# Gate arithmetic in a PSUM bank, reciprocals in spare PSUM columns, and another order of all steps, in a fused sparse-attention and mixture-of-attention-experts kernel

## The chip, the cores and the metric

The kernel runs on one core of a Trainium2 chip. A core has five engines with their own instruction queues: TensorE (matmuls, PE in the profile, its weight loads PEld), VectorE (DVE), ScalarE (ACT), GpSimd (POOL) and SyncE (SP). Here SP issues the loads of v and the stores of the output, and GpSimd issues the loads of q, k and the weights. Matmul results land in PSUM, which has eight banks of 512 float32 columns on 128 partitions; GpSimd works on SBUF only in this kernel. The metric is the device time of one launch in microseconds (us); lower is better.

## The reference

Two stages. The first is an attention for 4 batches, 8 heads, 768 positions and 64 columns, in which each query sees its neighbours within 16 positions and 24 block summaries (the maximum of k and the mean of v over blocks of 32). Its output, seen as 768 rows of 512 columns per batch, is the input x of the second stage: four attention experts, of which each row uses the two with the largest gate logits.

```python
k_sum = k.reshape(B, H, nb, block, D).max(axis=3)
v_sum = v.reshape(B, H, nb, block, D).mean(axis=3)
scores_l = scale * np.matmul(q, k.transpose(0, 1, 3, 2))      # kept where |i - j| < 16
scores_s = scale * np.einsum('bhsd,bhnd->bhsn', q, k_sum) + np.log(block)
# softmax over both, times [v, v_sum]
...
logits = x @ w_gate                                           # (B, S, 4)
topk = np.argpartition(-logits, K, axis=-1)[..., :K]          # K = 2
w = softmax of the two selected logits
for e in range(E):
    q, k, v = x @ wq[e], x @ wk[e], x @ wv[e]
    a = causal softmax of scale * q @ k.T
    ye = a @ v @ wo[e]
    out += (weight of expert e in each row) * ye
```

## The kernel before

Every piece of work is a step with a name, a function that issues its instructions, and the buffers that it reads and writes. `make_plan` lists the steps; `TABLE` is an order written out by hand: one entry per step with its number, its engine (P, V, A, G, S for TensorE, VectorE, ScalarE, GpSimd, SP) and the slots of the buffers that are new in it. `emit` issues the steps in that order, so each engine works through its own steps in the order of the table, and a step waits for data and for buffers. The durations beside each step (`{"V": 0.65}`) take no part in what is issued.

Names carry batch, pair of heads or of experts, and part. First stage, for batch b and pair of heads c (16 times): dk, dq, dv load (lines 285, 303); kz zeroes the spare rows of the three `kn` buffers (line 214); tk and tq transpose k and q on TensorE (line 393); rk takes the block maxima (410), kw and cq copy the transposed k and q out of PSUM, ksc appends the maxima; bs and be sum v over blocks (322, 340) and ds spreads the sums into `vb`, and hc copies v's overlapping halves; for four groups of heads (`TREE`), tr does the sums by additions on GpSimd (367, 370), on the buffer `vt` that vtz zeroes once; sc makes scores (435 the mask, 441 the product), ex exponentiates (449), av multiplies with v (459), rc and xm divide, tx transposes (486), hi and lo split the result into two half-precision parts (503 is lo).

Second stage, for each batch: vp multiplies x with the values' weights and the gate's (554, 557) for two of six row blocks at a time, lg copies the eight gate columns out to `lgp`, v2 copies the values out; then the gate, on 24 numbers per partition: ga (583 to 586) joins the logits' two parts, takes the maximum and subtracts; gx exponentiates on ScalarE (590); gb (595 to 598) finds the second largest and a mask; gc (603 to 606) makes the weights. All of these work in the SBUF buffer `gt`. For each pair of experts cc: pp makes q and k (622), pc copies them out, sp makes scores in six units (646), es exponentiates (654), dm zeroes the upper triangle on GpSimd (659), aw multiplies with the values (670). Then r2 (689, 691) takes the reciprocal of the softmax sum and multiplies it with the gate's weight, wv scales the result into `wav` (696), tw transposes (708), ct copies to `wT`, op multiplies with the output weights (728), oc copies out and od stores (739). The last batch splits r2 to ct into row blocks 0 to 3 and 4 to 5.

PSUM buffers are numbered slots of one tensor of eight banks; most second-stage buffers take two neighbouring banks. Some steps have a filler in front of them (`f...`): three matmuls on zeros in the same bank, issued if the table gives it to P and left out if it gives N.

The gate's weight columns hold two parts: `cg` (533 to 536) rounds the gate weights to half precision and stores the remainder times `LO_SCALE` (2048).

Of the kernel before, what the change touches and what calls it, by code (L numbers as in the profile page):

```python
# [55 lines left out]
95,A, 92,P,0 96,A, 115,P,1 45,N,2 98,P,0 117,V, 46,P,2 33,N,5 119,V, 50,V, 247,G,0 49,V, 99,A, 248,G,2 47,V, 34,P,1
35,V, 54,N,0 120,N,2 259,G,0 51,N,6 32,A, 68,P,4 28,A, 17,S,2 66,N,5 55,P,1 56,A, 103,N,0 12,V, 52,P,2 137,G, 53,A,
118,G, 136,G, 14,G, 67,P,0.1 36,A, 71,V, 69,P,2 19,N,6 20,P,0 21,V, 121,P,3 100,P,6 140,G, 73,A, 72,G, 122,A, 138,G,
22,G, 15,G, 74,N,2 101,P,4 70,V, 313,P,4.1.0 37,S,3 75,P,5 438,G,1 433,S,0 104,P,0.0 434,G, 139,G, 435,G,0 249,S,4
18,V, 102,A, 77,N,6 24,A, 78,P,0 315,A, 79,A, 39,N,5 40,P,1 142,V, 105,P, 41,V, 42,A, 316,V, 269,N,6 270,P,0.2  # L60
59,P,4.1.1 57,N, 106,V, 107,V, 274,V, 58,P, 60,V, 292,N,7 61,V, 76,A, 123,N,0 16,V, 124,P,4 293,P,2.1 297,V, 275,A,
62,N,4 63,P,0.0 38,A, 125,A, 296,V, 64,A, 80,N,2 108,N,0 109,P,1.1 110,V, 111,V, 82,P,1.2 81,P, 294,P,7 65,V,
126,N,0 127,P,0.0 273,A, 128,P, 331,P,6.0 83,V, 251,S,5 84,V, 129,V, 130,V, 295,P,2 299,A, 271,N,7 85,N,4 159,N,2
86,P,2.2 87,A, 88,V, 131,N,0 132,P,3.3 133,A, 134,V, 335,V, 272,P,1 276,A, 277,N,4 160,P,0 280,N,0 281,P,1 282,A,
161,V, 278,P,2 162,N,6 169,N,0 163,P,1 164,V, 317,A, 279,A, 330,P,2.0.2 333,V, 332,A, 314,P,3.1 318,V, 143,N,6
144,P,0.0 146,V, 439,G,1 427,G,0 145,V, 165,N,4 166,P,0 167,A, 321,P,2.0 322,A, 170,P, 334,A, 171,A, 253,N,6 254,P,0
298,G, 255,V, 181,N,4 303,N,2 304,P,5 177,N,0 178,P, 300,N,6 301,P,3 256,V, 305,A, 151,N,2 152,P, 302,A, 179,A,
154,A, 153,V, 185,N,6 186,P, 252,G, 436,G,1 187,A, 338,P,0.4 339,A, 173,N,2 182,P, 174,P, 257,V, 307,P,6.1.1 175,A,
262,S,2 250,V, 306,P, 308,V, 309,V, 483,P,0.2.0 486,V, 183,A, 485,V, 336,P,2.5 337,A, 310,P,6.4.4 311,V, 319,P,4.3
444,S,0 188,G, 500,P,1.0.2 445,G, 320,A, 200,N,2 201,P,2 197,N,4 198,P,0 312,V, 487,V, 260,S,0 219,N,6 202,V, 199,A,  # L70
147,N,2 264,N,0 503,V, 265,P,1 180,G, 266,V, 502,A, 220,P,1 221,A, 148,P, 484,P,4.2 267,V, 449,P,5.1.1 285,P,0.0.2
172,G, 268,A, 150,V, 452,V, 453,V, 283,N, 284,P, 451,A, 263,G, 341,P,6.1.0 340,P, 488,V, 149,A, 211,N,4 446,G,1
428,G,2 450,P,2.0 454,A, 286,V, 287,V, 501,P,3.1 212,P, 489,P,0.1 342,V, 343,V, 447,G,3 505,V, 344,P,6.5.5 345,V,
491,P,2.2 213,A, 346,V, 261,G, 323,P,4.1.1 324,P, 490,A, 492,A, 455,P,6.4 456,A, 325,V, 326,V, 288,N,0 289,P,6.6
290,V, 457,P,2.5 458,A, 223,N,6 224,P, 327,P,4.7.7 207,N,2 208,P, 225,A, 291,V, 328,A, 209,A, 467,P,6.2 471,V,
466,P,7.2.0 168,G, 597,G,2 329,V, 504,G, 469,V, 448,G,5 215,N,0 216,P, 203,N,2 636,P,6.1.1 639,V, 176,G, 217,A,
204,P, 362,P,4.1 470,A, 363,V, 360,P,0.0 431,S,4 155,V,0 184,G, 205,A, 389,P,4.2 598,G,0 468,A, 474,P,2.3 156,A,
361,V, 440,S, 157,V, 614,S,0 640,G, 189,P,0.0.0 141,G, 432,G, 390,V, 158,V, 191,P, 190,P, 192,V, 638,A, 367,P,4.0
193,V, 475,A, 472,P,6.0 368,A, 364,P,0 441,G, 494,P,2.0.2 493,P, 473,A, 365,A, 437,G, 506,P,4.2 495,V, 496,V,
620,P,6.0 507,A, 619,P,7.2.2 379,P,0 621,V, 218,G, 370,P,2 380,A, 371,A, 381,G, 622,V, 376,P,4 377,A, 222,G, 624,V,  # L80
214,G, 347,P,0.1.1 349,A, 348,V, 353,P,2 497,P,4.0.0 355,V, 498,V, 206,G, 373,P,6 374,A, 499,V, 391,P,0.0 442,S,
443,V, 429,S, 369,G, 226,G, 210,G, 227,P,1.1.6 228,P, 392,A, 229,P, 230,V, 231,V, 354,A, 408,P,4.1 409,A, 393,P,0
396,P,6 402,P,2 394,A, 476,P,4.1.0 403,A, 397,A, 477,P, 601,S,2 430,G, 478,V, 479,V, 399,P,0 400,A, 350,P,2 352,V,
623,G, 351,V, 608,G,1 508,P,6.1 509,A, 404,G, 480,P,4.1.1 627,P,0.0 628,A, 609,G,1 481,V, 482,V, 405,P,2 406,A,
460,P,6.0.1 459,P, 461,V, 462,V, 670,P,0.0.0 672,A, 637,P,1.2 641,A, 232,N,4 233,P,0 234,V, 625,P,2.3 626,A, 673,V,
# [791 lines left out]
```

## Time and profile before

| What | us |
| --- | --- |
| Median of three runs | 203.48 (203.15 to 208.5) |
| Profiled execution, its own time | 205.5 |
| Its span, first to last instruction | 203.6 |
| First instruction to end of the first batch's last lo | 50.0 |
| End of the last projection (pp301) | 184.9 |

The span is divided among engines in busy time, and the same span is followed back from its last instruction as a chain: at each step to what released it. An instruction's wait is shown in brackets with its releaser. The tile `gt` is the gate's buffer; `wav` holds the scaled attention output; `ps` is PSUM; a line can be a helper's, such as 181 for any copy on VectorE or GpSimd and 179 for any on ScalarE.

### The profile page before, as it was taken

The page shows a single profiled execution, that of the slowest core. Times are in us where ns is not written, and L with a number is a line of the kernel's source. Part 1 is how long each engine was busy: PE and PEld are TensorE (multiplying, and loading weights), DVE is VectorE, ACT ScalarE, POOL GpSimd, SP SyncE. Part 2 cuts the span into 40 slices and gives each one's busy share as a digit, 9 for nine tenths or more (in the row PEclk, how much of TensorE's full clock was granted, in tenths as well). Part 3 has the DMA queues.
Part 4 walks back from the last instruction along what each step waited for, and adds up shares of the span by engine and source line. Part 5 has one row for each costly group of instructions (what it writes and reads, how often), then busy time and mean ns, then how long its engine had stood idle before and what let it go on. Part 6 is the DMA issues. An engine that isn't in the chain of part 4 may idle for free.

```text
span 203.6 us, 7088 instructions
## 1 busy us (share of the span) xinstructions
PE 160.1 (79%) x3071; PEld 117.2 (58%) x3071; DVE 133.2 (65%) x251; ACT 121.9 (60%) x158; POOL 100.1 (49%) x156
## 2 busy tenths in 40 slices
...
GB/s 46 201 207 178 191 173 73 77 209 140 83 198 172 16 3 159 187 205 163 122 3 3 77 85 105 164 284 46 11 95 3 3 3 310 3 3 0 217 215 190
DMA packets 44207, 23.54 MB, mean 116 GB/s; under 512 B 33168, under 2 KB 39568, under 8 KB 44176
## 3 DMA queue, kind: packets, MB, share of 16 engines
...
HBM read 24.13 MB, written 6.29 MB: 149 GB/s over the span
## 4 chain that ended last, share of the span: by engine, by line
PE 37%; DVE 23%; POOL 13%; DMA 13%; issue 6%; ACT 4%; SPq 1%; ACTq 0%; DVEq 0%; POOLq 0%
DMA vt<-in_v_dram 9%; PE ps L459 8%; PE ps L622 5%; PE ps L670 4%; PE ps L728 4%; PE ps L554 3%; DVE wav L696 3%; PE ps L646 3%; DMA qn<-in_q_dram 3%; POOL kn L214 3%; POOL vt L367 2%; DVE ks L410 2%; DVE kw L181 2%; PE ps L393 2%; PE ps L486 2%
## 5 line engine op out<-in xcount | busy, mean ns | idle before, releaser
L654 ACT ACTIVATE a<-ps 128x1024 f16<-128x1024 f32 (+1 forms) x48 | 42.6, 923 | 13.6 <-PE ps L646 10.1
L659 POOL TENSOR_SCALAR_AFFINE_SELECT a<-a 128x256 f16<-128x256 f16 x48 | 18.7, 415 | 59.1 <-ACT a L654 42.4
L449 ACT ACTIVATE aT<-ps 120x768 f32<-120x768 f32 x32 | 25.7, 813 | 19.0 <-PE ps L441 18.9
L459 PE MATMUL ps<-vb,aT 120*64 120x65 f32 x768 | 28.4, 233 | 0.8 <-DVE vs L340 0.3
L459 PEld LDWEIGHTS ps<-vb,aT 120*64 120x64 f32 x768 | 25.8, 146 | 4.2 <-issue 2.4
L622 PE MATMUL ps<-hi,wqk 128*128 128x384 f16 x128 | 23.9, 340 | 0.4 <-DVE lgp L181 0.4
L646 PE MATMUL ps<-qk,qk 64*128 64x512 f16 (+3 forms) x128 | 16.5, 320 | 9.2 <-DVE wav L696 6.6
L367 POOL TENSOR_TENSOR vt<-vt 120x1024 f32<-120x1024 f32 (+1 forms) x8 | 14.6, 1820 | 17.0 <-DMA vb<-in_v_dram 9.7
L410 DVE TENSOR_REDUCE ks<-ps 128x24 f16<-128x768 f16 x16 | 15.0, 948 | 10.0 <-PE ps L393 10.0
L179 ACT COPY kw<-ps 128x1152 f16<-128x1152 f16 x10 | 11.1, 1119 | 14.8 <-DVE ks L410 14.4
L435 PE MATMUL ps<-pi,mt 64*128 64x384 f16 x64 | 12.8, 377 | 7.4 <-DVE wav L696 5.0
L622 PEld LDWEIGHTS <-wqk 128*128 128x128 f16 x128 | 12.4, 101 | 9.8 <-issue 3.1
L503 DVE TENSOR_TENSOR lo<-ps,hi 128x768 f16<-128x768 f32 x16 | 15.0, 954 | 1.4 <-ACT hi L179 0.9
L474 DVE TENSOR_TENSOR x<-ps,rec 128x768 f32<-128x768 f32 x16 | 15.3, 957 | 0.5
L441 PEld LDWEIGHTS <-kw 64*128 64x128 f16 x384 | 12.1, 104 | 5.1 <-issue 3.2
L670 PE MATMUL ps<-v,a 128*128 128x65 f16 x336 | 13.0, 199 | 2.3 <-ACT ob L179 1.1
L670 PEld LDWEIGHTS <-a 128*128 128x128 f16 x336 | 12.5, 101 | 4.0 <-issue 2.8
L441 PE MATMUL ps<-qT,kw 64*128 64x64 f16 x384 | 13.3, 204 | 1.4 <-issue 1.4
L554 PE MATMUL ps<-wvg,hi 128*128 128x264 f16 x96 | 13.8, 275 | 0.5 <-DVE qk L181 0.3
L393 PE MATMUL ps<-ke,kn 100*64 100x100 f16 x256 | 9.5, 228 | 5.9 <-POOL kn L214 5.9
L181 POOL COPY vb<-vu 24x768 f32<-24x768 f32 x16 | 13.2, 823 | 0.8
L646 PEld LDWEIGHTS <-qk 64*128 64x128 f16 x128 | 5.8, 95 | 13.3 <-issue 11.3
(103 smaller groups left out, 307.0 us busy)
## 6 DMA issues: line engine op xcount, KB each, us to landing
...
out_dram<-ob SPq DMA_DIRECT2D x11, 512.0 KB, 4.0
...
out_dram<-ob SPq DMA_DIRECT2D x2, 256.0 KB, 2.2
...
```

The costliest lines, as they stand in the source:

```text
L181: en(e).tensor_copy(dst, src)
L367: en(e).tensor_tensor(c[:, 0:a], c[:, 0:a], c[:, a:2 * a], AL.add)
L410: nc.vector.tensor_reduce(T["ks"][ks.slot], view(pbank16(kp), 2, [[4, NSUM], [NP, 8], [1, 4]]), AX.XY, AL.max)
L441: nc.tensor.matmul(s[:, hp, 64 * t:64 * t + 64], T["kw"][kw.slot][r, tt, :], T["qT"][qT.slot][r].rearrange("d (s p) -> d s p", s=8)[:, :, ...
L449: nc.scalar.activation(T["aT"][aT.slot][0:KR], pbank(sc, 2)[0:KR, :, 0:384], AF.Exp, scale=SCALE)
L459: nc.tensor.matmul(pbank(av, 2)[o:o + 64, u, 65 * (2 * (t // 2) + hp):65 * (2 * (t // 2) + hp) + 65], a[0:KR, hp, 64 * t:64 * t + 64], T[" ...
L554: nc.tensor.matmul(p[:, i, 0:264], hi_(ch)[:, cols], T["wvg"][:, ch, :], start=(ch == 0), stop=False, skip_group_check=True)
L622: nc.tensor.matmul(pbank(pp, 2)[:, u, 0:384], T["wqk"][:, cc, ch, j, :], hi_(ch)[:, 384 * u:384 * u + 384], start=(ch == 0), stop=(ch == N ...
L646: nc.tensor.matmul(pbank(sp, 2)[:, ep, c0:c0 + w], T["qk"][qk[1].slot][r, 128 * tj:128 * tj + 128], T["qk"][qk[0].slot][r, n0:n0 + w], sta ...
L654: nc.scalar.activation(a2v(u), pbank(sp, 2)[:, :, 0:ln], AF.Exp, scale=SCALE / (XS * XS))
L659: nc.gpsimd.affine_select(m, m, [[0, 2], [1, 128]], AL.is_ge, 0.0, base=0, channel_multiplier=-1)
L670: nc.tensor.matmul(pbank(av, 2)[:, ep, 65 * ti:65 * ti + 65], a2v(u)[:, ep, o:o + 128], T["v2"][v2.slot][:, tj, 2 * cc + ep, :], start=(tj ...
```

## The change

Three things change.

The gate works in a PSUM bank (`gp`, one of the eight, in place of `lgp`, whose buffers go). lg becomes a VectorE reduction that adds the two parts of the logits as it takes them out of the matmul's bank, always on VectorE; for that, both parts must have the same scale, so the gate weights are multiplied by `GS` (64) once, in cg, and the remainder is stored as it is; gx divides by `GS` again. ga loses its first operation. gb and gc keep the masked logits, the masks and the products in the bank (`gw`), and what is read beside them in `gt`. The bank is taken by the first lg of a batch and free after gc.

r2 writes the reciprocals to columns 400 and up of the bank whose sums it reads, and the product with the gate's weight to `cmb`.

The table is new from end to end: the same 778 steps, in another order, some on other engines and in other slots. On VectorE instead of GpSimd are kz, vtz, and ds00, ds20, ds30, ds32; instead of ScalarE among others kw02, kw03, ds01, ds02, ds03. On ScalarE instead of VectorE are among others kw00, kw01, kw22, kw30, kw32, and the qk casts pc001, pc011, pc100, pc101, pc110. GpSimd has cg, ds10, ds12, hc00, hc23, hc31, hc32, hc33 in place of VectorE. Six fillers are issued in place of five.

The queues' beginnings and ends in the new order:

```
GpSimd: dk010 dq010 id16 dk001 dq001 dk000 ke dk110 dq000 dq110 dwk0 mt dk210 sel dwq0 id32 dwv hc00 ...
VectorE: zz v2o vz vone kz rk02 pi rk03 kwz kw02 kw03 be03 rk01 ksc01 ds03 ksc02 cq01 be01 rk00 rc03 xm03 ds01 vtz ...
SP: dv03 dv01 dv02 dv00 dv13 dwg ...
TensorE: fillers, tk02 tk03 tq03 tq02 bs03 sc031 tk01 sc030 tq01 bs01 tk00 av031 av030 ...
TensorE at the end: ... pp301 op22 sp300 sp301 op21 sp303 vp31 sp302 sp304 vp32 vp30 sp305 op20 aw312 aw302 aw300 aw310 aw311 tw301 tw311 aw301 op32 tw310 tw300 op33 op30 op31
```

and in the old one:

```
GpSimd: dk010 dk000 dq010 dq000 dk001 dq001 ke kz id16 sel dk110 mt dk100 ...
VectorE: zz vz rk02 kwz be01 pi rk00 rk03 cq03 cq00 ksc00 kw00 be02 vone ...
SP: dwg dv01 dv02 dv00 dv03 ...
TensorE: fbs01 ftq03 tk00 tk02 tk03 bs01 tq02 tq03 sc020 tq00 bs02 ...
TensorE at the end: ... pp301 tw200 tw210 sp303 sp300 sp304 op22 op21 sp302 aw311 aw310 op20 aw300 aw301 sp305 tw310 tw300 sp301 op31 aw312 op30 aw302 tw301 tw311 op33 op32
```

On VectorE the gate stands, before: `gc0 r2000 wv000`, `gc1 r2100 wv100`, `gc2 r2200 wv200`, `gb3 oc22 gc3 r2310 wv310`; after: `gc0 rk11 kw11 cq21 r2000 wv000`, `r2010 wv010 ... gc1 oc00 ... r2110 wv110`, `gc2 rc30 xm30 ... r2210 wv210`, `gc3 r2301 r2311 wv301`.

The diff without the table:

```diff
-LO_SCALE = 2048.0
+GS = 64.0
...
         def cg(e):
             w = en(e)
+            w.tensor_scalar(T["wg32"], T["wg32"], GS, None, AL.mult)
             w.tensor_copy(T["wvg"][:, :, 256:260], T["wg32"])
             w.tensor_copy(T["wgt"], T["wvg"][:, :, 256:260])
-            w.tensor_tensor(T["wgt"], T["wg32"], T["wgt"], AL.subtract)
-            w.tensor_scalar(T["wvg"][:, :, 260:264], T["wgt"], LO_SCALE, None, AL.mult)
+            w.tensor_tensor(T["wvg"][:, :, 260:264], T["wg32"], T["wgt"], AL.subtract)
...
-        v2, lgp, gt = R.buf("v2"), R.buf("lgp"), R.buf("gt")
+        v2, gp, gt = R.buf("v2"), R.buf("ps"), R.buf("gt")
+
+        def gw(i):
+            return pbank(gp)[:, 0, 24 * i:24 * i + 24].rearrange("p (t e) -> p t e", e=4)
...
             def lgc(e, t2=t2, vp=vp):
-                copy(e, T["lgp"][lgp.slot][:, 2 * t2:2 * t2 + 2, :], pbank(vp, 2)[:, :, 256:264])
-            R.step(f"lg{b}{t2}", {"V": 0.16, "A": 0.18}, [vp], [lgp], lgc)
+                w = pbank(vp, 2)
+                nc.vector.tensor_reduce(gw(0)[:, 2 * t2:2 * t2 + 2, :].unsqueeze(3),
+                                        w[:, :, 256:264].rearrange("p t (h e) -> p t e h", h=2),
+                                        AX.X, AL.add)
+            R.step(f"lg{b}{t2}", {"V": 0.2}, [vp], [gp], lgc)
...
         def ga(e):
-            w = en(e)
-            lgv = T["lgp"][lgp.slot]
-            nc.vector.scalar_tensor_tensor(g4(0), lgv[:, :, 4:8], 1.0 / LO_SCALE, lgv[:, :, 0:4],
-                                           AL.mult, AL.add)
-            nc.vector.tensor_reduce(g1(1), g4(0), AX.X, AL.max)
-            w.tensor_tensor(g4(2), g4(0), bc(g1(1)), AL.subtract)
+            nc.vector.tensor_reduce(g1(1), gw(0), AX.X, AL.max)
+            nc.vector.tensor_tensor(g4(2), gw(0), bc(g1(1)), AL.subtract)
...
         def gb(e):
-            w = en(e)
-            w.tensor_tensor(g4(4), g4(0), bc(g1(1)), AL.is_ge)
-            nc.vector.scalar_tensor_tensor(g4(4), g4(4), -1e12, g4(0), AL.mult, AL.add)
-            nc.vector.tensor_reduce(g1(1), g4(4), AX.X, AL.max)
-            w.tensor_tensor(g4(4), g4(0), bc(g1(1)), AL.is_ge)
+            nc.vector.tensor_tensor(g4(4), gw(0), bc(g1(1)), AL.is_ge)
+            nc.vector.scalar_tensor_tensor(gw(1), g4(4), -1e12, gw(0), AL.mult, AL.add)
+            nc.vector.tensor_reduce(g1(1), gw(1), AX.X, AL.max)
+            nc.vector.tensor_tensor(gw(1), gw(0), bc(g1(1)), AL.is_ge)
...
         def gc(e):
-            w = en(e)
-            w.tensor_tensor(g4(4), g4(3), g4(4), AL.mult)
-            nc.vector.tensor_reduce(g1(1), g4(4), AX.X, AL.add)
+            nc.vector.tensor_tensor(gw(2), g4(3), gw(1), AL.mult)
+            nc.vector.tensor_reduce(g1(1), gw(2), AX.X, AL.add)
             nc.vector.reciprocal(g1(1), g1(1))
-            w.tensor_tensor(g4(5), g4(4), bc(g1(1)), AL.mult)
+            nc.vector.tensor_tensor(g4(5), gw(2), bc(g1(1)), AL.mult)
...
                 def r2(e, cc=cc, avv=avv, cm=cm, i0=i0, i1=i1, av=av):
                     t = T["cmb"][cm.slot][:, :, i0:i1, :]
-                    nc.vector.reciprocal(t, avv()[:, :, i0:i1, 64:65])
+                    w = pbank(av, 2)[:, :, 400 + i0:400 + i1].unsqueeze(3)
+                    nc.vector.reciprocal(w, avv()[:, :, i0:i1, 64:65])
...
-                    nc.vector.tensor_tensor(t, t, g, AL.mult)
+                    nc.vector.tensor_tensor(t, w, g, AL.mult)
```

More of the change, by code (lines that the diff above doesn't have):

```diff
@@ L49 @@
 SLOTS = dict(qn=3, kn=3, ks=3, kw=3, qT=3, aT=6, x32=2, vb=6, vs=2, vt=1, vu=2,
-             rec=3, hi=8, lo=8, v2=2, lgp=2, gt=2, qk=3, a2=2, cmb=2, wav=2,
+             rec=3, hi=8, lo=8, v2=2, gt=2, qk=3, a2=2, cmb=2, wav=2,
              wT=4, ob=3)
 TABLE = """
-29,G,0 1,G,1 135,S, 0,V, 112,N,0 25,P,1 89,N,2 30,G,0 2,G,1 3,G, 4,G, 114,P,3 43,N,4 11,V, 23,S,0 6,G, 7,G, 44,P,0.0
-90,P,1.1 94,V, 91,N,5 31,S,1 5,G, 113,P,2.2 9,V, 93,A, 13,G, 116,A, 258,G,2 10,G, 26,P,0 27,V, 97,N,6 8,V, 48,V,
@@ L56 @@
[L56 to L85, printed above, removed]
@@ new lines @@
+60,V, 261,G, 105,P,4.0.0 61,V, 103,N, 104,P, 134,V, 500,P,0.1.2 336,P,2.2 339,A, 141,G, 106,V, 337,A, 263,G, 107,V,
+502,A, 62,N,6 63,P,2.2 64,V, 317,V, 108,N,2 109,P,3.3 110,A, 65,V, 321,P,4.0 322,A, 264,N,1 111,V, 159,N,6 160,P,0
+161,V, 251,S,1 162,N,4 163,P,1 265,P,1 266,V, 165,N,2 173,N,6 164,A, 174,P,0 175,A, 503,V, 504,A, 166,P, 167,A,
+151,N,4 152,P,0 181,N,6 182,P, 183,A, 253,N,1 254,P,0 268,G, 154,A, 147,N,2 177,N,6 178,P, 153,V,0 143,N,4 144,P,
+433,S,0 148,P, 250,A, 179,A, 185,N,6 255,V, 145,V, 269,N,1 184,G, 267,G, 146,V, 168,G, 319,P,4.1 149,V, 176,G,
@@ new lines @@
+150,V, 252,G, 270,P,2.1 274,V, 324,P,2.1.1 180,G, 320,A, 323,P, 325,V, 326,V, 273,A, 155,V,0 156,A, 292,N,1 169,N,4
+157,V, 170,P, 186,P, 187,A, 197,N,2 188,G, 171,A, 172,G, 158,V, 293,P,0.0 297,V, 198,P,2 199,A, 296,V, 200,N,6
+201,P,0 202,A, 189,P,0.0.4 203,N,2 190,P, 467,P,0.0 471,V, 204,P,1 207,N,6 208,P, 191,P, 434,G, 205,A, 192,V,
+340,P,0.0.2 215,N,2 216,P, 209,A, 210,G, 439,G,2 219,N,6 193,V, 298,A, 217,A, 435,G,0 220,P, 221,A, 271,N,4 597,G,1
+300,N,2 257,V, 294,N,5 295,P,1 299,V, 272,P,2 218,G, 276,A, 341,P, 342,V, 343,V, 301,P,3 302,A, 303,N,6 304,P,5
@@ new lines @@
+393,P,4.0 640,A, 394,A, 402,P,2 214,G, 228,P,1.1.6 227,P, 403,A, 454,V, 445,G, 229,P, 446,G,1 447,G,5 399,P,4 400,A,
+430,G, 230,V, 231,V, 484,P,1.1 405,P,2 406,A, 395,G, 396,P,4 397,A, 453,G, 360,P,6.2 408,P,2 409,A, 361,A, 488,V,
+491,P,4.3 492,A, 410,G, 401,G, 353,P,2 354,V, 355,V, 432,V, 489,P,6.5 448,G,4 490,A, 440,S, 232,N,4 233,P,1
+466,P,1.2.0 457,P,2.0 350,P,6 234,A, 608,G,0 239,N,4 240,P,0 469,V, 351,V, 356,V,1 352,A, 357,A, 458,A, 243,N,6
+244,P,1 362,P,2.0 468,A, 470,G, 241,V, 437,G, 245,A, 358,V, 359,V, 363,A, 441,G, 235,N,4 236,P,2 442,S, 237,V,
@@ L107 @@
+712,G, 691,V,2 694,V, 688,V, 696,V,1 697,A, 698,V, 719,P,0 720,A, 588,P,4.1 757,P,0.0.6 589,A, 709,G, 721,G, 699,V,
+724,P,1.1.0 729,V, 762,V, 722,P, 730,V, 763,V, 755,P, 756,P, 758,V, 731,P,4.2 764,P,2.3 765,V, 596,S, 590,S, 759,V,
+723,P, 732,A, 772,P,2.0 773,A, 774,S, 725,V, 726,V, 760,P,6 727,P,4 761,V, 728,V, 775,P,3.2 776,V, 777,S, 766,P,0.1
+767,A, 768,S, 769,P,6.0 770,A, 771,S,
 """
```

68 lines of the change are left out of this document (40 added, 28 removed).

## The prediction

> **What bounds the kernel now.** I read the page first (engines, chain), then busy time by stretch, then the waits of TensorE, then the timeline where TensorE stands longest, and last the rows of single tiles.
>
> ```profile
> span 203.6 us, 7088 instructions
> PE 160.1 (79%) x3071; PEld 117.2 (58%) x3071; DVE 133.2 (65%) x251; ACT 121.9 (60%) x158; POOL 100.1 (49%) x156
> ...
> PE 37%; DVE 23%; POOL 13%; DMA 13%; issue 6%; ACT 4%; SPq 1%; ACTq 0%; DVEq 0%; POOLq 0%
> ```
>
> No engine is full. TensorE is the busiest, but it is only 37% of the chain that ended last; VectorE has 23% of it and GpSimd with the transfers 26%. So the time is 160 us of matmuls plus some 43 us in which TensorE stands still, and the question is which of those the change takes away.
>
> ```profile
> 11.40:50.10 38.70, 31.41 (x669) 23.77 (x665) 28.88 (x60) 25.52 (x30) 22.18 (x38) 1.00 1.21 155
> 50.10:184.90 134.80, 113.18 (x2200) 84.77 (x2201) 94.50 (x164) 83.22 (x111) 64.82 (x96) 0.92 0.56 95
> 184.90:203.60 18.70, 11.26 (x173) 6.35 (x172) 8.16 (x25) 11.88 (x16) 3.06 (x8) 0.92 0.44 169
> ...
> PE ps L646 <- DVE wav L696: 6.6, 5, 1.9
> PE ps L435 <- DVE wav L696: 5.0, 1, 5.0
> ```
>
> The columns of the first three rows are stretch, length, busy TensorE, weight loads, VectorE, ScalarE, GpSimd, granted clock, transfers. Idle TensorE is 7.3 us up to 50.1, 21.6 us in the long middle, 7.4 us in the tail, and the rest before 11.4. In the middle its largest wait has one name: `wav`, the scaled attention output (11.6 us in six waits). `wav` comes from VectorE step wv, which follows r2, which needs the gate's weights from gc. So the gate lies right ahead of the largest wait of the largest engine. The timeline shows why it is slow:
>
> ```profile
> 92.98 2.87 POOL L181 COPY vb<-vb 32x1536 f32<-32x1536 f32 x2
> 92.99 1.48 DVE L586 TENSOR_TENSOR gt<-gt 128x24 f32<-128x24 f32 x1
> ...
> 95.26 0.61 DVE L595 TENSOR_TENSOR gt<-gt 128x24 f32<-128x24 f32 x1
> 95.90 1.69 POOL L181 COPY vb<-vu 24x768 f32<-24x768 f32 x2
> 95.91 0.85 DVE L596 SCALAR_TENSOR_TENSOR gt<-gt 128x24 f32<-128x24 f32 x1
> ...
> 131.24 2.36 POOL L367 TENSOR_TENSOR vt<-vt 120x1024 f32<-120x1024 f32 x1 [4.29 <-DMA vt<-in_v_dram]
> 131.97 1.66 DVE L595 TENSOR_TENSOR gt<-gt 128x24 f32<-128x24 f32 x1
> 134.27 1.27 POOL L367 TENSOR_TENSOR vt<-vt 120x512 f32<-120x512 f32 x1
> 134.53 1.06 DVE L603 TENSOR_TENSOR gt<-gt 128x24 f32<-128x24 f32 x1
> 137.95 0.51 PE L435 MATMUL ps<-pi,mt 64*128 64x384 f16 x2 [5.02 <-DVE wav L696]
> ...
> L586 DVE TENSOR_TENSOR gt<-gt x4: 183/184/1481, 93.0 to 179.1; 128x24 f32<-128x24 f32 x4
> L595 DVE TENSOR_TENSOR gt<-gt x4: 172/395/1659, 95.3 to 186.2; 128x24 f32<-128x24 f32 x4
> L596 DVE SCALAR_TENSOR_TENSOR gt<-gt x4: 182/252/847, 95.9 to 186.4; 128x24 f32<-128x24 f32 x4
> L597 DVE TENSOR_REDUCE gt<-gt x4: 179/179/179, 96.8 to 186.7; 128x6 f32<-128x24 f32 x4
> L603 DVE TENSOR_TENSOR gt<-gt x4: 166/254/1058, 98.4 to 188.8; 128x24 f32<-128x24 f32 x4
> ```
>
> Columns: start, length; in the last rows shortest, median and longest of the four batches. The same instruction on the same 24 elements takes 0.17 us or 1.66 us, and the long ones end where GpSimd's instruction beside them ends: L595 at 133.63, GpSimd's at 133.60; L603 at 135.59, GpSimd's at 135.54. L597 reads one tensor only, and it takes 179 ns each time. So a gate operation that reads two tensors from SBUF waits for the GpSimd instruction that is under way. The five instances cost 1.30 + 0.44 + 0.67 in batch 0 and 1.49 + 0.89 in batch 1, 4.8 us in all.
>
> **The change part by part.**
>
> *Gate in PSUM.* Each lg step now adds the logits' high and low part in one VectorE reduction into a bank, so ga loses its first operation (L583). Every two-tensor operation of ga, gb and gc, and the product in r2, then has one operand in PSUM and at most one in SBUF. By the rows above, that takes away the 4.8 us of holding, wherever GpSimd is at work. What it is worth depends on cover. In batch 1, wv waits for the gate and TensorE stands 5.02 us until that wv: the 2.4 us there I take whole. In batch 0 VectorE carried casts of qk between the gate's operations, and three of those (pc110, pc100, pc101) move to ScalarE in the new order; I take 0.4 of the 2.4. That is -2.8. Ends: -4.8 if all of it shows; if the new order has other work late at those places, nothing, and +0.5 for what PSUM operands may cost. To price that:
>
> ```profile
> L181 DVE COPY lgp<-ps x7: 164/174/175, 56.0 to 172.5; 128x16 f32<-128x16 f32 x7
> ...
> L536 DVE TENSOR_SCALAR wvg<-wgt x1: 174/174/174, 31.9 to 31.9; 128x16 f16<-128x16 f32 x1
> ...
> L689 DVE RECIPROCAL cmb<-ps 128x12 f32<-128x12 f32 x6 | 1.4, 229 | 7.3 <-PE ps L670 7.3
> ...
> L605 DVE RECIPROCAL gt<-gt 128x6 f32<-128x6 f32 x4 | 0.8, 194 | 0.1
> ```
>
> Sixteen elements from PSUM take 174 ns and sixteen from SBUF 174 ns: no surcharge. The upper bound is 229 - 194 = 35 ns, all put down to PSUM though one reads twice the elements. Some nine operations a batch become PSUM readers, 36 in all, so 0 to 1.3 us of VectorE time; a third of it on the path gives the +0.5. I take 0.
>
> [...]
>
> The lg steps that were ScalarE copies (five of 12, about 0.17 us each) go to VectorE; they stand behind vp, beside other matmuls, and cost nothing while VectorE is at 65%. If that cover were gone, 0.9 us. The reordered scale in cg (GS on the weights, once) goes from VectorE to GpSimd, before vp needs it by many steps: nothing.
>
> *r2.* The reciprocal goes to spare columns of the same bank that it reads, no wait is added, the product no longer meets GpSimd: the same row kinds, nothing more.
>
> *The head.* The zeroing of kn's spare rows (kz) and of vt (vtz) move from GpSimd to VectorE, id16 and ke come before more loads, sel comes behind the load dk210.
>
> ```profile
> 0.93 0.27 DVE L744 MEMSET zz<- 128x256 uint32 x1 [0.93 <-PEq L861]
> 6.28 5.29 POOL L214 MEMSET kn<- 4x2048 f16 x3
> 9.87 2.21 PE L393 MATMUL ps<-ke,kn 100*64 100x100 f16 x48 [5.87 <-POOL kn L214]
> 11.46 0.96 DVE L410 TENSOR_REDUCE ks<-ps 128x24 f16<-128x768 f16 x1 [8.65 <-PE ps L393]
> 16.25 1.00 DVE L232 COPY pi<-id 64x384 f16<-64x384 f16 x2
> 16.79 1.00 PE L435 MATMUL ps<-pi,mt 64*128 64x384 f16 x2 [0.44 <-DVE pi L232]
> ...
> DMA to landing us min/median/max: 5.9/6.3/6.7
> ...
> L181 DVE COPY kw<-ps 128x1152 f16<-128x1152 f16 x6 | 8.0, 1341 | 0.5 <-PE ps L393 0.5
> ```
>
> Now GpSimd zeroes for 5.29 us and both other engines wait. On VectorE, 2048 half-words are 1024 words, four times the zz row: 4 x 0.27 = 1.1 us at most, three of them 3.3 us, inside its 8.65 us of idling. Then the landing of the first k load ends last: issued at some 1.4, landed 6.7 later (the landing row is that of the first two k loads), 8.1. One transpose step is a third of 2.21, so rk02 starts near 8.85 instead of 11.46: -2.6. From there VectorE runs rk, pi, rk, the small kwz and two kw copies, 0.96 + 1.00 + 0.96 + 0.2 + 2 x 1.34 = 5.8, and the first score matmul comes at 14.7 or so against 16.79: -2.1. I take -2.3. On GpSimd's queue dk210 waits for tk02 and tk03 to free its buffer, and sel and dwq0 wait behind it; bs03 waits for sel, and be03 for bs03, but VectorE reaches be03 only after the two kw copies. On SP's queue the first v loads stay first and the gate's weights fall behind five of them; vp is far off. Ends: until the last lo of batch 0 the new VectorE queue holds some 4 us more work (ds03, ds01, ds02, ds00 and vtz come in; hc00, cg and one rk and kw go), while the old one had 38.7 - 28.9 = 9.8 us of idle there. If all idle shrinks as the start does, -5; if that work is simply added to a start 2.6 sooner, +1.5.
>
> *The middle.* All other steps change place. The engine changes nearly balance by count: kw two to VectorE and five away, ds seven to it and two away, hc one to it and six away, qk casts three and five, output copies two and one. With the held gate operations gone VectorE's sum falls by some 5 us, while TensorE's work, 160 us, is the same but for one more filler. No row says that one order suits the chip better, so 0; the ends are plus and minus 3, about an eighth of the 21.6 us that TensorE idles there.
>
> *The tail.* Three vp steps of batch 3 now stand behind pp301 instead of before it; that lets pp301 end earlier by what it adds behind: 0 net. The last outputs change: before, two single blocks went last, now op30 and op31, two blocks each.
>
> ```profile
> out_dram<-ob SPq DMA_DIRECT2D x11, 512.0 KB, 4.0
> ...
> out_dram<-ob SPq DMA_DIRECT2D x2, 256.0 KB, 2.2
> ```
>
> The final transfer lands 1.8 us later after its issue. Against it, only one last pair of blocks has to be copied behind the last matmul, and ct300 comes on VectorE while ScalarE is free. I take +0.8, ends -1 and +2.7.
>
> Sum: -2.3 - 2.8 + 0 + 0.8 = -4.3. The profiled execution took 205.5 us in its own time, a span of 203.6 and 1.9 around it; it would become 201.2. The median of the runs shown is 203.48, 2.0 below the profiled one, so 199.2 on that scale.
>
> **The rivals.**
>
> *The gain is given back (203).* The gate is freed, but wv then waits for its attention matmuls, or the new head, with 4 us more on VectorE, reaches the projections no sooner. For it: the chain has many short members, no one of them large. Against: the longest single wait of TensorE goes straight through the gate. With the gate's -2.8 lost, the head at -1.3 and the tail at +0.8, 203.0.
>
> *PSUM operands are dearer than I take them (200.0).* At 35 ns by the upper row, 36 of them cost 1.3 us of VectorE time; at the gate's own places, with twice that price, a third of 2.5 gives +0.8 and 200.0. Against: 174 ns from PSUM and from SBUF. [...]
>
> *Slower: the gate's bank starves TensorE (208).* The gate's bank is held from the first lg to gc. In batch 1 that is from lg10 to gc1, over 21 TensorE steps: sp110 to sp115, three aw, two vp, two pp and three sc among them, most of which want pairs of banks out of seven. Where such a step finds no pair, TensorE stands as it did at 133 to 138, for 5.02 us, and behind the stop it runs slow: the 0.51 us of that L435 pair. Two such stops and the lost gain of the gate give 199.2 + 10 less the 1 or so of cover, 208. For it: TensorE's largest wait now is already one for banks that wv frees. Against: in batches 0, 2 and 3 the hold spans only 8, 5 and 3 TensorE steps, and the order was laid out with the bank counted as taken. It decides from some 8 us of new waiting.
>
> **How the numbers follow.** A measurement of this kernel can tell about 2% from no change: faster is under 199.4, slower over 207.6. The forecast case has 0.46 and lies just inside faster. Given back has 0.27 and dearer PSUM 0.11, both within 2%: 0.38. The bank case has 0.16. All ends together on the good side, -5, -4.8, -3, -1, would be 189.7, and never fall together; a little over half of them gives 194.5. Upwards, 206.0 takes in given back and half of the way to the bank case. The likeliest case alone runs from 195.5 to 202.
>
> **What would show it.** Right: no gate or cmb operation above 0.3 us in any batch; the first L410 near 9 us and L214 on VectorE; TensorE's waits for wav well under 11.6 us; VectorE's sum near 127. Wrong: gate operations still held beside GpSimd; first score matmuls at 16.8 or later; a TensorE stop of several us whose releaser frees a bank between lg10 and gc1; an end that waits over 4 us for the last output.

## The result, and the profile after

The changed kernel takes 191.5 us (median of four runs, 190.61 to 193.45) against 204.5 us for the kernel before beside it: a ratio of 0.940, 95% interval 0.928 to 0.952. That is faster, some 12 to 13 us, and below the lower end of the predicted range (194.5). The ratio compares the faster runs of each kernel, so it is not quite that of the two medians. Two later measures of the same kernel gave 0.942 and 0.952 (below), so the gain is known as 10 to 13 us. The profiled execution took 190.61 us with a span of 188.7.

First the page of the changed kernel (engines; the granted clock in 40 slices; chain), then its busy time in the same three stretches as in the prediction: up to the end of the first batch's last lo, up to the end of pp301, and the tail. The columns are those explained there.

```profile
span 188.7 us, 7092 instructions
PE 157.0 (83%) x3074; PEld 113.9 (60%) x3074; DVE 130.5 (69%) x253; ACT 121.2 (64%) x153; POOL 98.9 (52%) x155
...
PEclk9965589969999999999999999999999999999879
...
PE 44%; DVE 21%; ACT 14%; DMA 9%; issue 6%; POOL 3%; ACTq 1%; DVEq 0%; POOLq 0%
...
11.40:49.20 37.80, 28.98 (x653) 23.75 (x654) 29.42 (x51) 22.98 (x27) 19.94 (x34) 0.78 1.37 176
49.20:164.80 115.60, 105.12 (x2149) 77.51 (x2148) 82.54 (x150) 85.44 (x109) 66.67 (x91) 1.00 0.54 104
164.80:188.70 23.90, 16.33 (x196) 9.42 (x194) 10.43 (x32) 11.23 (x16) 3.87 (x10) 0.92 0.36 133
```

The whole gain is in the middle. The first batch's last lo ends at 49.1 instead of 50.0. The middle is 115.6 us instead of 134.8: TensorE's idle time there falls from 21.6 to 10.5 us, and its busy time from 113.2 to 105.1. Of that last fall, 5.1 us is work that only moved into the tail (11.3 to 16.3 us busy, and the tail is 5.2 longer); the other 3 us goes with the clock, which was 0.92 in the middle and is 1.00. GpSimd, 13% of the chain before, is 3% of it now.

Two views show what became of the gate: TensorE's waits between 49 and 165 us (total, times, longest), and the rows of the gate's operations (shortest, median, longest of the four batches).

```profile
PE ps L647 <- ACT a L655: 1.5, 2, 0.9
PE ps L441 <- DVE qT L181: 1.3, 1, 1.3
PE ps L730 <- ACT wT L179: 1.1, 1, 1.1
...
L597 DVE TENSOR_TENSOR gt<-ps,gt x4: 172/172/173, 64.2 to 173.1; 128x24 f32<-128x24 f32 x4
L598 DVE SCALAR_TENSOR_TENSOR ps<-gt,ps x4: 186/186/189, 64.4 to 173.3; 128x24 f32<-128x24 f32 x4
L604 DVE TENSOR_TENSOR ps<-gt,ps x4: 186/189/189, 65.1 to 174.0; 128x24 f32<-128x24 f32 x4
...
L693 DVE TENSOR_TENSOR cmb<-ps,gt x10: 161/170/174, 69.5 to 178.8; 128x12 f32<-128x12 f32 x6, 128x4 f32<-128x4 f32 x2, 128x8 f32<-128x8 f32 x2
```

The waits for wav, 11.6 us in six before, are gone from the head of the list; its largest entry is now 1.5 us (whether the gate or the order took them away is asked below). No VectorE operation of the gate takes more than 0.2 us in any batch, and not because GpSimd was out of the way, as the timeline of batch 2's gate shows (start, length):

```profile
136.33 3.08 POOL L181 COPY vb<-vb 32x1536 f32<-32x1536 f32 x2
137.69 0.17 DVE L588 TENSOR_REDUCE gt<-ps 128x6 f32<-128x24 f32 x1
137.89 0.18 DVE L589 TENSOR_TENSOR gt<-ps,gt 128x24 f32<-128x24 f32 x1
137.99 0.17 DVE L597 TENSOR_TENSOR gt<-ps,gt 128x24 f32<-128x24 f32 x1
138.20 0.19 DVE L598 SCALAR_TENSOR_TENSOR ps<-gt,ps 128x24 f32<-128x24 f32 x1
```

GpSimd copies from SBUF to SBUF from 136.33 to 139.41, and three two-tensor operations, each with one operand in PSUM, run beside it in 0.17 to 0.19 us. L595 took 1.66 us beside GpSimd before, with both operands in SBUF; L597, the same comparison with one of them in PSUM, takes 0.17 us here.

### The profile page after: what moved, and what is told of

Same layout as the page of the kernel before. It is cut to its first block, busy times and chain, and to the rows that moved or that the text cites. A ratio compares the mean times of both kernels' runs of the same rounds, so it can differ in the third digit from the quotient of the medians.

```text
span 188.7 us, 7092 instructions
## 1 busy us (share of the span) xinstructions
PE 157.0 (83%) x3074; PEld 113.9 (60%) x3074; DVE 130.5 (69%) x253; ACT 121.2 (64%) x153; POOL 98.9 (52%) x155
## 4 chain that ended last, share of the span: by engine, by line
PE 44%; DVE 21%; ACT 14%; DMA 9%; issue 6%; POOL 3%; ACTq 1%; DVEq 0%; POOLq 0%
PE ps L623 9%; PE ps L459 8%; DMA wvg<-in_moe_wv_dram 5%; ACT a L655 5%; DMA qn<-in_q_dram 4%; PE ps L730 4%; PE ps L647 4%; PE ps L558 4%; ACT kw L179 3%; DVE vb L181 3%; DVE ks L410 3%; DVE x L474 3%; DVE lo L503 3%; PE ps L393 3%; PE ps L671 2%
## 5 line engine op out<-in xcount | busy, mean ns | idle before, releaser
L623 PE MATMUL ps<-hi,wqk 128*128 128x384 f16 x128 | 23.0, 327 | 1.4 <-DVE lo L503 0.5
L181 POOL COPY vb<-vb 32x1536 f32<-32x1536 f32 x11 | 16.4, 1501 | 8.0 <-DMA vb<-in_v_dram 7.6
L179 ACT COPY kw<-ps 128x1152 f16<-128x1152 f16 x13 | 14.4, 1118 | 9.5 <-DVE ks L410 9.0
L647 PE MATMUL ps<-qk,qk 64*128 64x512 f16 (+3 forms) x128 | 15.7, 308 | 2.8 <-ACT a L655 1.5
L367 POOL TENSOR_TENSOR vt<-vt 120x1024 f32<-120x1024 f32 (+1 forms) x8 | 14.7, 1841 | 5.1 <-DMA vt<-in_v_dram 4.9
L441 PE MATMUL ps<-qT,kw 64*128 64x64 f16 x384 | 12.1, 197 | 3.0 <-DVE qT L181 1.3
L730 PE MATMUL ps<-wo,wT 128*128 128x512 f16 x48 | 13.3, 406 | 1.5 <-ACT wT L179 1.1
L441 PEld LDWEIGHTS <-kw 64*128 64x128 f16 x384 | 10.7, 99 | 6.1 <-issue 2.9
L671 PEld LDWEIGHTS <-a 128*128 128x128 f16 x336 | 11.5, 97 | 4.3 <-issue 3.3
L179 ACT CAST qk<-ps 128x768 f16<-128x768 f32 x11 | 8.9, 806 | 6.5 <-PE ps L623 5.7
L322 PE MATMUL ps<-vb,sel 64*32 64x128 f32 x208 | 9.4, 307 | 4.3 <-POOL sel L266 3.5
```

Of the source, the lines that this page charges most:

```text
L179: nc.scalar.copy(dst, src)
L181: en(e).tensor_copy(dst, src)
L441: nc.tensor.matmul(s[:, hp, 64 * t:64 * t + 64], T["kw"][kw.slot][r, tt, :], T["qT"][qT.slot][r].rearrange("d (s p) -> d s p", s=8)[:, :, ...
L623: nc.tensor.matmul(pbank(pp, 2)[:, u, 0:384], T["wqk"][:, cc, ch, j, :], hi_(ch)[:, 384 * u:384 * u + 384], start=(ch == 0), stop=(ch == N ...
L647: nc.tensor.matmul(pbank(sp, 2)[:, ep, c0:c0 + w], T["qk"][qk[1].slot][r, 128 * tj:128 * tj + 128], T["qk"][qk[0].slot][r, n0:n0 + w], sta ...
L671: nc.tensor.matmul(pbank(av, 2)[:, ep, 65 * ti:65 * ti + 65], a2v(u)[:, ep, o:o + 128], T["v2"][v2.slot][:, tj, 2 * cc + ep, :], start=(tj ...
```

## The experiments

The prediction gave the gate's bank 2.8 us and the order of the steps nothing. So the first question was how the 12 us divide between the two. Ratios are to the kernel before, run beside each, with 95% intervals.

**The new order with the gate in SBUF (e1, f1).** Masks and products get an SBUF tensor of their own; r2's reciprocal goes to `cmb` again. The bank stays reserved, and the order and engines are those of the changed kernel.

```diff
-            return pbank(gp)[:, 0, 24 * i:24 * i + 24].rearrange("p (t e) -> p t e", e=4)
+            return T["gw"][b % 2][:, i, :, :]
...
-                    w = pbank(av, 2)[:, :, 400 + i0:400 + i1].unsqueeze(3)
+                    w = t
```

> The new order and engines with the gate's working tiles and r2's reciprocals in SBUF again (the bank stays reserved). Theory A (held gate operations were the loss): the two-operand gate operations are held by GpSimd again, TensorE stops ahead of wv and runs at half clock behind the stop, so 3 to 6 us over the changed kernel's 191.5, 195 to 198. Theory B (the order was the loss): the gate stands 3.8, 13 and 18 us ahead of the first wv of batches 0 to 2 in the new order, so holds are hidden there: within 1 us of 191.5, even if single gate operations take over 0.5 us.

**The old order with the gate in PSUM (e2, f2).** Batches 0 to 2 keep logits, masks and products in columns 432 and up of banks that are free there; batch 3 stays in SBUF. Everything else is the kernel before, but for the scale GS, the reduction that now joins the logits' parts in ga, and r2's spare columns.

```diff
+GBANK = [4, 0, 6]
...
+        def gw(i):
+            if b == B - 1:
+                return g4((0, 4, 4)[i])
+            c = 432 + 24 * i
+            return T["ps"][:, GBANK[b], c:c + 24].rearrange("p (t e) -> p t e", e=4)
```

> The old order with the gate of batches 0 to 2 working in spare columns of PSUM banks, and r2's reciprocals as in the change; batch 3's gate stays in SBUF. Theory A: 4.8 us of holds go, and with them most of the stops at 94 to 98 and 133 to 138 and some of the half-clock stretches behind them: 195 to 199. Theory B: the gate is still issued late and right ahead of wv, and VectorE brings its other steps in the same order: 201 to 203.

e1 took 194.62 us, 0.956 [0.947, 0.965], and e2 197.04 us beside 203.56. So the holds cost time in the new order too, and taking them away helps in the old one (theory A of both expectations, though e1 came out just under its 195). To compare them, both were run again on one chip with the changed kernel (f0):

> The changed kernel, for a comparison with the next three on one chip: 190 to 192.

> The new order with the gate in SBUF again, now beside the changed kernel. If holds cost time in the new order too (5.4 us of them in its first profile), 2 to 4 us over the changed kernel, with intervals apart. If they are hidden there, as a gate that is issued late and met few of them (192.9) may say, under 1 us.

> The old order with the gate in PSUM again: if the holds and the half clock behind their stops cost over half of the change, 195.5 to 198 and a ratio near 0.965; if its first measure was low by chance, 199 to 201.

| | gate in SBUF | gate in PSUM |
| --- | --- | --- |
| old order | 1 (before, median 203.4 us) | f2: 0.963 [0.956, 0.970] |
| new order | f1: 0.968 [0.960, 0.977] | f0: 0.952 [0.944, 0.959] |

Each alone is worth 3 to 4%, and by the table together they make less than their sum: the gate's bank brings 3.7% in the old order and 1.7% in the new one (the intervals of f1 and f0 lie just apart), the order 3.2% with the gate in SBUF (4.4% in e1's runs) and 1.1% with it in PSUM (there the intervals overlap). That they overlap is less sure than that each is worth something: f2's 0.963 rests on two of its six runs, 192.8 and 193.4 us, and the other four took 198.0 to 198.8. By the medians of all runs f1 is 0.959, f2 0.975 and f0 0.941, so the bank brings 2.5 and 1.7%, the order 4.1 and 3.3%, and little is counted twice. In f1 the gate is held as before (rows of its tile), and the middle and the tail show where that costs; f0's middle row stands last:

```profile
L598 DVE SCALAR_TENSOR_TENSOR gw<-gt,gw x4: 183/759/1490, 65.4 to 178.5; 128x24 f32<-128x24 f32 x4
L600 DVE TENSOR_TENSOR gw<-gw,gt x4: 183/208/1161, 65.9 to 179.0; 128x24 f32<-128x24 f32 x4
...
50.10:170.10 120.00, 105.19 (x2150) 77.73 (x2149) 88.74 (x151) 85.77 (x109) 66.44 (x91) 1.00 0.52 100
170.10:193.10 23.00, 15.25 (x196) 9.08 (x194) 10.19 (x32) 11.23 (x16) 3.89 (x10) 0.94 0.37 138
```

```profile
49.20:165.00 115.80, 105.77 (x2153) 77.89 (x2152) 83.27 (x151) 86.13 (x110) 66.77 (x91) 1.00 0.55 105
```

Between f1 and f0 the middle shrinks by 4.2 us: TensorE's idle time by 4.8 (14.8 to 10.0), its busy time hardly, the clock not at all. That is the gate's bank in the new order. Between the kernel before and f1 (order, engines, slots, and lg with its scale) the middle shrinks from 134.8 to 120.0: idle time by 6.8 us, busy time by 8.0, of which 4.0 reappears in the tail and the rest goes with the clock, 0.92 to 1.00. That is the order, with the engines and slots that it brings.

The waits for `wav` divide otherwise than the prediction had it. TensorE's waits with `wav` as releaser, in f2 (old order, gate in PSUM) and then in f1 (new order, gate in SBUF), from 45 to 187 us:

```profile
PE ps L649 <- DVE wav L700: 5.7, 5, 1.7
PE ps L712 <- DVE wav L700: 1.5, 2, 0.9
PE ps L436 <- DVE wav L700: 0.8, 1, 0.8
```

```profile
PE ps L671 <- DVE wav L698: 0.8, 1, 0.8
PE ps L710 <- DVE wav L698: 0.8, 1, 0.8
PE ps L393 <- DVE wav L698: 0.2, 1, 0.2
```

Of 11.6 us, f2 keeps 8.0 without one hold in batches 0 to 2, and f1 keeps 1.8 with nine holds above 0.3 us. The bank ends the one stop of 5.0 us; most of the other waits for wav go only with the order. In the changed kernel the gate ends 3.8, 12.9 and 18.3 us ahead of the first wv of batches 0 to 2, where it ended 0.4 to 0.6 us ahead of it before. So in the new order a held gate hardly costs through wav. It costs through what stands behind it on VectorE (timeline of f1; f0 has neither wait):

```profile
110.01 0.39 PE L647 MATMUL ps<-qk,qk 64*128 64x512 f16 x2 [2.42 <-DVE ob L181]
...
146.76 0.23 PE L647 MATMUL ps<-qk,qk 64*128 64x128 f16 x2 [1.44 <-DVE x L474]
```

The output copy starts at 108.75, right behind batch 1's held gate (up to 108.82), and rc and xm at 145.50, right behind batch 2's (up to 145.58). The two waits make 3.9 of the 4.2 us.

**The gate earlier, in SBUF (e3).** Each batch's ga, gx, gb and gc stand right behind its last lg, in the old order. If only the gate's lateness cost time, this should bring it.

```diff
-    R.emit(decode(TABLE))
+    R.emit(moved(decode(TABLE), [(155, 149, False), (156, 155, False), ...]))
```

> The old order, gate in SBUF, but ga, gx, gb and gc of each batch issued right behind the batch's last lg, ahead of other VectorE work. Theory A: the operations are still held by GpSimd, somewhere else: 202 to 205. Theory B in its narrow form (it was the gate's place ahead of wv that cost): the stops of TensorE ahead of wv at 98 and 138 shrink to under 2 us and the clock does not halve behind them: 194 to 199.

209.24 us, 1.026 [1.015, 1.038]: slower, and outside what either theory expected. Who waited for the gate's tile in e3 (total, times), and TensorE's waits from 50 to 187 us (total, times, longest):

```profile
  ACT gt L590: 6.5, 4
...
PE ps L646 <- DVE wav L696: 7.8, 5, 2.8
PE ps L459 <- ACT aT L449: 2.9, 1, 2.9
```

The stop of 5.02 us is gone, and fewer operations are held (7 above 0.3 us, against 12 before, counted over all instructions on `gt` and `cmb`). But gx now stands early in ScalarE's queue and waits there for ga, 6.5 us in four batches against 1.2 us in one before; the exponentials behind it come later, and TensorE waits for one of them, 2.9 us. That these waits are the whole loss is not shown; the early gate at least brought nothing here.

**The gate late, in SBUF (e10).** e1 with gb and gc of batches 0 to 2 right ahead of r2, and without the bank.

```diff
-        v2, gp, gt = R.buf("v2"), R.buf("ps"), R.buf("gt")
+        v2, gp, gt = R.buf("v2"), R.buf(".gp"), R.buf("gt")
...
+    R.emit(moved(decode(TABLE), [(157, 192, True), (158, 192, True), ...]))
```

> The new order with the gate in SBUF (194.6), and gb and gc of batches 0 to 2 right ahead of the batch's first r2 on VectorE, as they stand in the old order. If the lead of the gate over r2 in the new order is what hides the holds (3.8, 13 and 18 us), 196 to 199. If the lead is worth nothing, 194 to 195.5, the same as with the gate early.

192.92 us, 0.943 [0.934, 0.951], better than either side of the expectation. Its longest gate operation took 0.449 us, and three on `gt` and `cmb` took over 0.3 us, against nine in f1: at those places few of GpSimd's instructions meet it. As far as runs on different chips compare (0.956 and 0.968 for e1 and f1; 0.940, 0.942 and 0.952 for the changed kernel), most of what the bank brings in the new order can be had without it, by placing. Whether the freed bank helped too is not separated.

**The price of a stop (e9).** In the kernel before, TensorE stands from 132.9 to 137.95 and is slow behind it. e9 fills that stop with 20 matmuls on zeros, into a bank that nobody holds; nothing is removed.

```diff
+                if (b, c, u) == (3, 2, 0):
+                    for _ in range(20):
+                        nc.tensor.matmul(T["ps"][:, 2, :], T["zz"][:, 0:128], T["zz"], start=True, stop=True)
```

> The old order and gate, with 20 filler matmuls of 512 columns on TensorE in front of sc320, so that TensorE works through its stop of 5.0 us at 133 to 138 instead of standing. If the half clock from 135.8 to 142.7 is the price of that stop and not of something else, it goes, and the matmuls behind the stop run at full speed: 2 to 3 us faster than before, about 200.5 to 201.5. If the clock costs nothing because ScalarE and VectorE bound the stretch, within 0.7 us of before.

201.31 us, 0.986 [0.978, 0.994]: useless work makes the kernel some 2.8 us faster. The timeline of TensorE, of e9 and then of the kernel before:

```profile
132.43 4.48 PE L434 MATMUL ps<-zz 128*128 128x512 f16 x20
...
137.62 1.45 PE L673 MATMUL ps<-v,a 128*128 128x65 f16 x42
```

```profile
139.35 2.49 PE L670 MATMUL ps<-v,a 128*128 128x65 f16 x42
```

The same 42 matmuls take 1.45 us behind fillers and 2.49 behind the stop. The granted clock of the kernel before, in stretches of 4 us through the stop, with e9's third stretch behind it:

```profile
134.00:138.00 4.00, 0.05 (x2) 0.04 (x3) 3.57 (x9) 0.00 (x0) 3.70 (x6) 0.73 1.04 324
138.00:142.00 4.00, 4.00 (x72) 3.43 (x72) 0.05 (x1) 2.43 (x3) 1.49 (x4) 0.50 0.21 25
```

```profile
138.00:142.00 4.00, 2.72 (x46) 1.67 (x43) 1.37 (x3) 2.72 (x4) 1.88 (x3) 1.00 0.08 9
```

In 138 to 142 TensorE is busy without a gap at 0.50, while VectorE, with 0.05 us of work, waits for it. The trace puts that slow stretch at 6.8 us. The edit shortens no hold, but in the profile of e9 the first one happens to be shorter (L595's comparison takes 0.89 us), and the stop lies 0.6 us sooner. Counted from the end of wv, the next wait for wav ends 4.2 us later in e9 and 5.9 us later before: that 1.7 us of the gain lies behind the stop.

The kernel before has three more such stretches between 50 and 184 us:

```profile
81.30:84.60 3.30, 3.30 (x66) 2.87 (x64) 2.21 (x3) 2.70 (x4) 2.37 (x5) 0.50 1.34 171
98.30:105.10 6.80, 5.70 (x90) 4.34 (x91) 3.02 (x10) 2.94 (x4) 0.00 (x0) 0.50 0.56 59
135.90:142.60 6.70, 4.43 (x72) 3.47 (x72) 2.51 (x7) 2.43 (x3) 3.97 (x7) 0.50 0.45 103
180.30:183.60 3.30, 3.30 (x12) 1.36 (x11) 0.03 (x1) 1.05 (x2) 0.77 (x2) 0.50 0.02 5
```

The second and third begin inside a stop of TensorE (1.7 and 5.0 us), the first and fourth up to 1.0 us behind one (2.0 and 1.9 us). Together they are 20.5 us long, with TensorE busy for 16.7 us in these rows. The same matmuls take 1.5 to 1.7 times as long there (4.18 us against 2.77 for 16 of L622, 2.49 against 1.45 for 42 of L670), so the four cost some 5.5 to 7 us of TensorE's time, an estimate from these rows. In the changed kernel, and in f1, the middle has none: 1.00 throughout. What makes the clock halve is not shown beyond e9, where the filled stop has no slow stretch. The length of a stop does not give the length of the stretch here: 6.8 us goes with the stop of 1.7 us as with that of 5.0, and 3.4 us with those of 1.9 and 2.0.

**The new engines in the old order (e6).** e2 with 71 steps on the engines that the new table gives them; kz, vtz, lg and the fillers excepted.

```diff
-    R.emit(decode(TABLE))
+    R.emit(moved(decode(TABLE), engines=[...]))
```

> The old order with the gate in PSUM (197.0), and every step on the engine that the new table gives it (71 steps, among them five qk casts from VectorE to ScalarE; not kz, vtz, fillers, lg). Theory C (what is left of the gain is the split of work among engines): 191 to 194. Theory D (it is the order itself, in which batch 0's second stage starts earlier): not better than 196, perhaps slower, since the order was laid out for other engines.

243.52 us, 1.208 [1.198, 1.217]. GpSimd and TensorE wait (total, times, longest):

```profile
POOL vb L182 <- DVE vs L341: 30.7, 2, 18.5
...
PE ps L460 <- POOL vb L182: 19.7, 2, 16.8
```

A step that changes its engine joins another queue at its place in the table, and there it can stand in front of what came earlier for a good reason. In the old order the new engines alone make the kernel 21% slower.

**The head (e5, e7, e8, e11, f3).** The prediction gave 2.3 us to kz on VectorE. e5 moves kz alone, in the old order; e7 also moves the load dk110 behind dq100:

```diff
-    R.emit(decode(TABLE))
+    R.emit(moved(decode(TABLE), engines=[(7, 'V')]))
...
+    R.emit(moved(decode(TABLE), moves=[(258, 248, False)], engines=[(7, 'V')]))
```

> The old order with the zeroing of kn's spare rows on VectorE instead of GpSimd, nothing else. If the head's gain of the prediction holds (first block maxima near 9 us instead of 11.5), some 2 us: 201 to 202. Rival: the first batch's results come no sooner, since later loads, sel and the kw copies end last, as in the changed kernel, whose first score matmuls came at 16.4 against 16.8: within 0.5 us of before.

> As the old order with kz on VectorE (207.6), but the load dk110 issued behind dq100, so that it leaves GpSimd after 12 us again instead of at 7.5. If the 4 us lost there came from that early load taking the transfers of v (TensorE waited 4.1 us for v at 22.8), 201 to 204. If moving kz itself costs, it stays at 206 to 208.

e5: 207.63 us, 1.023 [1.014, 1.031]; e7: 209.89 us, 1.040 [1.032, 1.048]; both are slower than either expectation allowed. Zeroing is quick on VectorE (0.91 us for each of three, against 5.29 for all on GpSimd) and the first maximum starts 0.6 us sooner, but GpSimd, now free, issues its loads sooner (dk110 at 7.46 us instead of 12.90), and the sums over v come later (timeline of e5, e5's busy time, and two rows of e7's timeline):

```profile
10.84 0.96 DVE L410 TENSOR_REDUCE ks<-ps 128x24 f16<-128x768 f16 x1 [4.70 <-PE ps L393]
22.84 1.91 PE L322 MATMUL ps<-vb,sel 64*32 64x128 f32 x26 [4.08 <-DMA vb<-in_v_dram]
...
11.40:26.00 14.60, 8.58 (x119) 5.88 (x117) 8.12 (x20) 7.06 (x8) 8.55 (x14) 1.00 1.25 192
...
18.77 1.91 PE L322 MATMUL ps<-vb,sel 64*32 64x128 f32 x26
27.99 1.88 PE L322 MATMUL ps<-vb,sel 64*32 64x128 f32 x26 [2.01 <-DMA vb<-in_v_dram]
```

In e5 TensorE waits 4.08 us for v, and it is busy for 8.58 us of that stretch, where the kernel before has 12.18. That q's and k's transfers had pushed v back was my theory for it. e7, which holds one such load back, bears it out for that one wait, since the sum starts at 18.77 as it did before (18.81); but the next sum then waits 2.01 us for v, the first batch's last lo ends at 54.1 (e5 54.9, before 50.0), and the kernel is no faster. What holds v back there stays open. e8 puts sel ahead of dk110 in the changed kernel; e11 puts nine filler matmuls in front of bs03, where TensorE waits for sel; f3 is e11 again, beside f0, and e0 the changed kernel beside e8. The diff shows e8's move and, below it, e11's longer filler.

```diff
+    R.emit(moved(decode(TABLE), moves=[(13, 258, True)]))
...
-        for _ in range(3 if e == "P" else 0):
+        for _ in range(n if e == "P" else 0):
```

> The changed kernel once more, beside the others of this call: 190 to 193, and with the gate in SBUF at 194.6 some 3 us slower than it.

> The changed kernel with sel ahead of the load dk110 on GpSimd, so that bs03 need not wait 3.5 us for sel at 14.5. If the head is bound by the queue of GpSimd, 1 to 3 us better, 189 to 190.5. If it is bound by the loads of v, k and q, no change: 191 to 192.

> The changed kernel with the filler fbs03 right in front of bs03 and nine matmuls long, so that TensorE works through its wait of 3.5 us for sel at 11.0 to 14.5. If the half clock from 11.0 to 24.7 costs time, 1 to 2 us better than the changed kernel, 189.5 to 190.5. If the loads and VectorE bound the first 45 us, the same within 0.7 us.

> The changed kernel with fillers in front of bs03 again: 0.5 us under the changed kernel if the shorter half clock at the start is worth what the first measure said (190.5 against 191.1), or the same.

e8: 192.17 us, 0.952 [0.945, 0.960], against e0's 191.06, 0.942 [0.935, 0.949]. e11: 190.54, 0.936 [0.930, 0.942]; f3: 191.28, 0.952 [0.946, 0.958], the same as f0's 0.952. TensorE's sum for bs03 and what follows it, in the changed kernel and in e8:

```profile
14.51 1.91 PE L322 MATMUL ps<-vb,sel 64*32 64x128 f32 x26 [3.47 <-POOL sel L266]
16.36 0.50 PE L435 MATMUL ps<-pi,mt 64*128 64x384 f16 x2
16.66 0.53 PE L441 MATMUL ps<-qT,kw 64*128 64x64 f16 x12
```

```profile
11.64 1.06 PE L322 MATMUL ps<-vb,sel 64*32 64x128 f32 x26
...
14.59 0.50 PE L441 MATMUL ps<-qT,kw 64*128 64x64 f16 x12 [0.67 <-DVE kw L181]
```

In e8 the first product of scores starts 2.1 us sooner, the first batch's last lo ends at 50.3 instead of 49.1, and the whole is no faster. This sooner start was worth nothing by itself. What paces the first 50 us is not settled; the page gives both kernels transfers at nine tenths or more in nearly all slices from 5 to some 50 us, and the changed one a slow TensorE (0.78 of the clock in 11 to 49 us); the old one's 1.00 in that stretch is no measurement up to 26.6 us (last section).

## Why the prediction was off

*The gate in PSUM, -2.8.* The holding was read rightly: with one operand in PSUM no gate or `cmb` operation takes over 0.3 us, beside GpSimd too (0.192 at the longest among the two-tensor ones). The size: in the new order the bank is worth 1.7%, about 3.4 us, near the 2.8, but that is luck: there the gate is far ahead of wv, and the 3.4 us come from an output copy and a division behind it; in the old one 3.7%, about 7.5 (2.5%, 5 us, by the medians). Two terms were left out of its price. I counted five held instances, 4.8 us; the trace has twelve above 0.3 us, and the other seven add 1.6. And I took 2.4 us of holding in batch 1 "whole" without the half clock behind the stop that they lengthen, although I had the slow 0.51 us row in my own fence and used it for the rival. e9 prices that stretch alone at 2.8 us [1.2, 4.5]. The sign that I named for it, the waits for wav well under 11.6 us, came true for another reason in the main: f1 has it without the bank, and f2, with the bank, keeps 8.0 us.

*PSUM's price, 0.* Right. At its shortest, the comparison (L595, now L597) takes 172 ns with one operand in PSUM and 172 with both in SBUF, the masked logits (L596, now L598) 186 against 182, and the product (L603, now L604) 186 to 189 against 166, so 23 ns at most. The rival of dearer PSUM operands falls: no run shows the twice 35 ns that it took for the gate's own places.

*r2, nothing.* Right: the product takes 174 ns at the longest, and in the kernel before it took 522 once.

*The head, -2.3.* The first maximum started at 8.30 (I had 8.85) and each zeroing took 0.91 us. Then the chain failed twice. I followed VectorE and let the first score product come at 14.7; TensorE's own queue has bs03 ahead of it, and that waited 3.47 us for sel, which now stands behind dk210 and which I had called harmless. The matmuls came at 16.36, against 16.79. And the worth of an early start was carried over one to one to the end of the stage: in the changed kernel the first batch's last lo ended 0.9 us sooner, and in e8, with the start 2.1 us sooner still, 0.3 us later than before.

*The middle, 0 with ends of 3.* This is the step that failed most, and the one that put the sum wrong: "No row says that one order suits the chip better, so 0" took lack of a row for a price. f1 shows 3.2% [2.3, 4.0], some 6.5 us, for the order with the gate held as before, and e1 4.4%, some 9; in f1's profile 6.8 us of it is idle time of TensorE and 4 us clock, less what the tail takes. The bound of 3 us was an eighth of the idle 21.6 us, without a reason for an eighth; half of it, -11, would have been as well founded. I had the clock row of the middle, 0.92, and read no price from it: 0.08 of 134.8 us is 10.8 us of lost clock at most, and the four half-clock rows make it 5.5 to 7, an estimate, of which 3 to 4 us show in TensorE's busy time. An order without these stops gets that back. And 11.6 us of waits for wav, which I put down to the gate, went with the order in the main (f1). Which of the moved steps bring it is open: in the old order the new engines alone make it worse (e6), kz alone does (e5), an early gate does (e3), and single steps were not tried further.

*The tail, +0.8.* Three vp behind pp301 made it 5.2 us longer, and TensorE has 5.1 us more to do there: net nearly nothing, as far as two profiles tell, and within the ends.

*VectorE's sum near 127.* It is 130.5. The bank does take off what I said (e1's page has 136.2, 5.7 more), but order and engines with the gate in SBUF add 3.0 to the 133.2 of before, where I had counted the engine changes as nearly balanced.

*The rivals.* Given back did not happen. Nor did the bank starve TensorE: after 49 us no row of its waits exceeds 1.5 us in sum, and the stop of 5 us is gone instead.
